# Pooled attention and two MoE layers in one kernel: turning the probabilities with one wide block transpose and moving the blocks by DMA

## Chip, cores and metric

One core of a Trainium2 chip runs the whole program. The metric is the device time of one execution in microseconds; the median of several runs is compared. All times below are microseconds (us) unless they are marked ns.

## What is computed

The reference, cut to what matters (B = 8 batches, H = 8 heads, S = 576 queries, D = 64, pool 8, so 72 pooled keys; 4608 tokens of 512 channels):

```python
k_p = k.reshape(B, H, Sp, pool, D).mean(axis=3)
v_p = v.reshape(B, H, Sp, pool, D).mean(axis=3)
scores = scale * np.matmul(q, k_p.transpose(0, 1, 3, 2))
scores = scores - np.max(scores, axis=-1, keepdims=True)
attn = np.exp(scores)
attn = attn / (np.sum(attn, axis=-1, keepdims=True) + 1e-09)
x = np.matmul(attn, v_p)            # to 4608 x 512
a = x @ w1                          # 512 -> 1024
b = x @ w2
x2 = ((a * b) @ w3) @ w_out         # 1024 -> 512
h = x2 @ w_in                       # 512 -> 2048
g = h * (1.0 / (1.0 + np.exp(-1.702 * h)))
out = g @ w_out2                    # 2048 -> 512
```

## The kernel before

**Numbers.** Every large product is made of three matmuls on rounded parts: each operand is split into a rounded high part and the rest (`split`, L104 on ACT for the high part, L105 on DVE or POOL for the rest), and `mm3` (L114, L115, L116) adds high·high, high·low and low·high. A "slot" `s` holds both parts of a 128x512 piece.

**Phases.** First w3 and w_out are folded into one matrix `wp`. Then the first MoE layer runs in 9 blocks of 512 tokens. A block has 8 steps f (128 hidden channels each): 24 matmuls for a = x@w1 and b = x@w2 into the PSUM banks `wk_70` and `wk_71`, an ACT copy of a (L638), DVE's a*b (L641), its split, and 12 matmuls of an older f into `acc`. At about 770 us the second MoE layer begins (L709), which this change does not touch.

**Attention** is cut into 32 groups n of two heads: four groups make one batch, and group 4b + c gives channel block c of the tokens of batch b. So f = 0 of the first block needs the outputs of groups 0 to 3, one `s` slot each (c = 0 to 3). A group passes through stages: `g0` (kT and qT by block transposes on DVE, L255/L256, and the pooled key sums L258), `g1` (scores on PE L278, row maximum L283 and subtraction L285 on DVE), `g2` (exp on ACT), `g3` (row sum L300, L301, L302, product L303 on DVE, and the turning L314), `g_va` (pooling of v on POOL, L324 to L332, and the load of the next v), `g_vb` (`vm`, `vt`, the two parts of the pooled v: ACT L338, POOL L339), `g4` (the two parts of the turned probabilities, `ph` and `pt`: ACT L368, L370, POOL L369, L372) and `g6` (PE: probabilities by v, eight matmuls of 288 columns; ACT L390 and DVE L391 copy the result as a slot of x).

In the stage `g3` the probabilities lie with 128 queries on the partitions, `s_t[128, 5, 160]`; PE needs the keys on the partitions. The first four groups (n < NPE = 4) are turned on PE in `g4` (L351 on). All others are turned on DVE by 20 block transposes of 32 partitions (L314), whose output goes to other partitions than the input:

```python
            for r in range(5):
                for c in range(4):
                    dst = p0[32 * r:32 * r + 32] if r < 4 else p1[:32]
                    nc.vector.transpose(out=dst[:, :nt, 32 * c:32 * c + 32],
                        in_=s_t[32 * c:32 * c + 32, :nt, 32 * r:32 * r + 32])
```

**What sets the order.** `tick_first` (groups 0 to 3, two ticks apart) and `tick` (four ticks a group) put the stages between the steps of the surrounding loops: the folding of wp first, then two ticks for each f of the blocks. Beside that runs `Conv`, which unpacks and rounds the weights of the second layer: its step (L155) uses ACT (L166, L168), DVE (L169), POOL (L172) and a split (L104, L105, tile `cv`). That written order is not the final one: a scheduler with a timeline of its own sets each engine's sequence when the program is built, so a change of one instruction can move others. Every engine then runs its sequence in order. The raw loads `kr`, `qr` (L229) and `vr`, `vtr` (L249, L250) are DMAs issued by SP. `vr` has one buffer, `vtr` is one fixed tile; `kr` and `qr` share four.

Of the kernel before, what the change touches and what calls it, by code (L numbers as in the profile page):

```python
# [22 lines left out]
def pooled_attention_moe_moe2(  # L23
# [167 lines left out]
    with pa_ctx:  # L191
# [104 lines left out]
        def g3(n):  # L296
# [20 lines left out]

        def g_va(n):

            vr, tr = g_v.pop(n), vtr  # L320
            a = pa.tile([P, 4 * D], F32, name="va", tag="va")
            at = pa.tile([32, 4 * D], F32, name="vat", tag="vat")
            for d, s in ((a, vr), (at, tr)):
                nc.gpsimd.tensor_tensor(out=d, in0=s[:, :4 * D], in1=s[:, 4 * D:], op=ALU.add)  # L324
                nc.gpsimd.tensor_tensor(
                    out=d[:, :2 * D], in0=d[:, :2 * D], in1=d[:, 2 * D:], op=ALU.add)
                nc.gpsimd.tensor_tensor(out=d[:, :D], in0=d[:, :D], in1=d[:, D:2 * D], op=ALU.add)
            vf = pa.tile([P, 2, D], F32, name="vf", tag="vf")
            nc.gpsimd.tensor_tensor(
                out=vf, in0=a[:, :D].unsqueeze(1).to_broadcast([P, 2, D]), in1=mask, op=ALU.mult)  # L330
            vtf = pa.tile([32, D], F32, name="vtf", tag="vtf")
            nc.gpsimd.tensor_scalar_mul(vtf, at[:, :D], 1.0 / POOL)  # L332
# [12 lines left out]
        def g4(n):  # L345
            p0, p1 = g_s.pop(n)
            if n < NPE:
                ps, s_t = banks_of(n), s_of(n)
                p0f, p1f = (t.rearrange("p t c -> p (t c)") for t in (p0, p1))
                for tt in range(4):  # L350
                    nc.tensor.transpose(ps[0][:, sl(tt)], s_t[:, tt, :P], ident)  # L351
                nc.scalar.copy(p0f[:, :T], ps[0])
# [13 lines left out]
            s0 = p0.rearrange("p t c -> p (t c)")[:, :S]  # L366
            s1 = p1.rearrange("p t c -> p (t c)")[:, :S]
            nc.scalar.copy(ph[:, 0], s0)  # L368
            nc.gpsimd.tensor_tensor(out=ph[:, 1], in0=s0, in1=f32(ph[:, 0]), op=ALU.subtract)  # L369
            nc.scalar.copy(pt[:32], s1)  # L370
            nc.scalar.copy(pt[32:64], s1)
            nc.gpsimd.tensor_tensor(out=pt[64:96], in0=s1, in1=f32(pt[:32]), op=ALU.subtract)  # L372
# [756 lines left out]
```

## Time and profile before

| | us |
|---|---|
| median of 3 runs | 1482.65 (1481.53 to 1482.81) |
| the profiled execution | 1480.04 |
| its span in the trace | 1478.3 |
| PE (TensorE matmul) busy | 1437.1 (97%), 6536 instructions |
| PEld (weight loads) | 1188.0 (80%) |
| DVE (VectorE) | 991.5 (67%), 1728 instructions |
| ACT (ScalarE) | 696.6 (47%) |
| POOL (GpSimd) | 491.9 (33%) |
| mean granted TensorE clock | 0.994 of full speed |

The profiled execution took 1480.04 us, of which the trace shows 1478.3; it is 2.6 us shorter than the median of the runs. In a timeline row the columns are the start, the busy time of the row, engine and line, output from input with the shape, and in brackets the idle time of the engine before it with what ended it; x6 means six instructions in one row. In a row of grouped instructions the columns behind the bar are the busy time, the mean ns of one, and the idle time before them. SP's entries (SPq) are the issues of DMAs.

### The profile page before, as it was taken

How to read it: one execution, taken by the hardware profiler on the slowest of the kernel's cores; microseconds unless marked ns; L12 is line 12 of the kernel's file. 1: busy time of each engine (PE TensorE's matmuls, PEld its weight loads, DVE VectorE, ACT ScalarE, POOL GpSimd, SP SyncE). 2: the span in 40 equal slices, each digit the busy share in tenths (PEclk: the TensorE clock that was granted, in tenths of full speed). 3: DMA queues.
4: the chain of work that ended last, by engine and by line, in shares of the span. 5: the costliest groups of instructions: out<-in, count | busy, mean ns of one | idle time of the engine just before them, and what ended most of it. 6: DMA issues, size and time to landing. Idle time of an engine off the chain costs nothing.

```text
span 1478.3 us, 19409 instructions
## 1 busy us (share of the span) xinstructions
PE 1437.1 (97%) x6536; PEld 1188.0 (80%) x6536; DVE 991.5 (67%) x1728; ACT 696.6 (47%) x1212; POOL 491.9 (33%) x589
## 2 busy tenths in 40 slices
PE   5978999999999999999999999999999999999998
PEld 3766888888888888888888887888788888888886
DVE  7889998878787877645636345783559354954554
ACT  6974444434343434366635334652455244634442
POOL 8787865555555555357743200000000000000000
PEclk9989999999999999999999999999999999999999
DMA  9992333323232321089869978877677766785665
GB/s 275 243 227 41 65 81 61 77 49 77 47 75 48 74 41 37 29 295 337 329 230 391 330 240 306 292 213 225 200 237 223 224 199 216 241 237 179 196 213 141
DMA packets 294434, 267.63 MB, mean 181 GB/s; under 512 B 201664, under 2 KB 226240, under 8 KB 294336
## 3 DMA queue, kind: packets, MB, share of 16 engines
q1 hardware_dynamic: 291648, 265.09, 60.0%
q10 hardware_dynamic: 2688, 1.31, 0.3%
q8 instruction: 52, 0.85, 0.2%
q14 instruction: 46, 0.38, 0.1%
HBM read 209.72 MB, written 56.62 MB: 180 GB/s over the span
## 4 chain that ended last, share of the span: by engine, by line
PE 82%; DVE 7%; DMA 5%; ACT 2%; POOL 2%; issue 1%; SPq 1%; DVEq 0%; ACTq 0%; POOLq 0%
PE bk L709 39%; PE wk L114 8%; PE wk L116 8%; PE wk L115 8%; PE acc L114 4%; PE acc L115 4%; PE acc L116 4%; PE wk L278 2%; DMA wud<-wt 2%; DVE s L105 1%; DVE cv L169 1%; PE bk L114 1%; PE bk L115 1%; PE bk L116 1%; POOL cv L172 1%
## 5 line engine op out<-in xcount | busy, mean ns | idle before, releaser
L709 PE MATMUL bk<-xM,st 128*128 128x512 f32 x1140 | 269.1, 390 | 1.8 <-DMA st<-wind 1.3
L709 PE MATMUL bk<-mv,st 128*128 128x512 f32 x1104 | 258.7, 389 | 0.5 <-DMA st<-wud 0.5
L709 PEld LDWEIGHTS bk<-xM,st 128*128 128x128 f32 x1140 | 213.6, 188 | 48.0 <-issue 1.9
L709 PEld LDWEIGHTS bk<-mv,st 128*128 128x128 f32 x1104 | 207.1, 188 | 44.2 <-ACT mv L104 0.9
L114 PE MATMUL wk<-s,s 128*128 128x512 f32 x576 | 227.3, 396 | 6.1 <-DVE a L641 4.1
L116 PE MATMUL wk<-s,s 128*128 128x512 f32 x576 | 225.2, 391 | 0.9 <-DVE s L105 0.9
L115 PE MATMUL wk<-s,s 128*128 128x512 f32 x576 | 225.3, 392 | 0.1
L314 DVE STREAM_TRANSPOSE p<-s_t 32x160 f32<-32x160 f32 (+1 forms) x560 | 178.3, 318 | 10.5
L115 PE MATMUL acc<-s,s 128*128 128x512 f32 x352 | 141.2, 401 | 1.0 <-POOL s L105 0.8
L116 PE MATMUL acc<-s,s 128*128 128x512 f32 x352 | 140.7, 400 | 1.6 <-DVE s L105 1.6
L114 PE MATMUL acc<-s,s 128*128 128x512 f32 x352 | 134.1, 406 | 8.1 <-DVE s L105 5.4
L114 PEld LDWEIGHTS wk<-s,s 128*128 128x128 f32 x576 | 108.5, 189 | 30.1 <-DVE a L641 5.4
L116 PEld LDWEIGHTS wk<-s,s 128*128 128x128 f32 x576 | 108.5, 188 | 23.8 <-DVE s L105 1.1
L115 PEld LDWEIGHTS wk<-s,s 128*128 128x128 f32 x576 | 108.5, 188 | 22.1 <-DVE s L391 0.5
L105 POOL TENSOR_TENSOR s<-a,s 128x512 fp32r<-128x512 f32 x56 | 73.3, 1309 | 155.2 <-ACT s L104 121.4
L105 DVE TENSOR_TENSOR mv<-g,mv 128x1024 fp32r<-128x1024 f32 x80 | 97.8, 1222 | 32.5 <-ACT mv L104 31.0
L104 ACT CAST mv<-g 128x1024 fp32r<-128x1024 f32 x80 | 84.5, 1056 | 71.3 <-PE bk L709 70.8
L172 POOL TENSOR_TENSOR cv<-cv,s 128x512 int32<-128x512 int32 x72 | 100.8, 1408 | 33.6 <-DVE cv L169 24.2
L114 PEld LDWEIGHTS acc<-s,s 128*128 128x128 f32 x352 | 67.9, 194 | 23.3 <-ACT s L104 4.7
L116 PEld LDWEIGHTS acc<-s,s 128*128 128x128 f32 x352 | 67.9, 193 | 15.8 <-DVE s L105 2.7
L115 PEld LDWEIGHTS acc<-s,s 128*128 128x128 f32 x352 | 68.0, 193 | 14.4 <-POOL s L105 2.0
L638 ACT COPY a<-wk 128x512 f32<-128x512 f32 x72 | 42.1, 585 | 68.3 <-PE wk L116 68.1
(188 smaller groups left out, 2344.6 us busy)
## 6 DMA issues: line engine op xcount, KB each, us to landing
st<-wud SPq DMA_DIRECT2D x92, 512.0 KB, 4.3
st<-wind SPq DMA_DIRECT2D x66, 512.0 KB, 4.6
st<-wind SPq DMA_DIRECT2D x84, 256.0 KB, 3.8
s<-in_moe_w_dram SPq DMA_DIRECT2D x32, 512.0 KB, 6.5
wind<-s SPq DMA_DIRECT2D x32, 512.0 KB, 5.5
s<-in_moe_w_out_dram SPq DMA_DIRECT2D x24, 512.0 KB, 6.9
s<-wud SPq DMA_DIRECT2D x20, 512.0 KB, 4.3
kr<-in_k_dram SPq DMA_DIRECT2D x128, 72.0 KB, 2.5
```

What stands on the lines that cost most here:

```text
L104: nc.scalar.copy(dst[:, 0], src)
L105: lo_eng.tensor_tensor(out=dst[:, 1], in0=src, in1=f32(dst[:, 0]), op=ALU.subtract)
L114: nc.tensor.matmul(o, a[:, 0, a_sl], b[:, 0, b_sl], start=first, stop=False)
L115: nc.tensor.matmul(o, a[:, 0, a_sl], b[:, 1, b_sl], start=False, stop=False)
L116: nc.tensor.matmul(o, a[:, 1, a_sl], b[:, 0, b_sl], start=False, stop=last)
L169: nc.vector.tensor_scalar(out=wu, in0=e.bitcast(U32), scalar1=3, scalar2=None, op0=ALU.logical_shift_left)
L172: nc.gpsimd.tensor_tensor(out=w.bitcast(I32), in0=w.bitcast(I32), in1=lo_w.bitcast(I32), op=ALU.add)
L278: nc.tensor.matmul(sc[half][:, i * KW:(i + 1) * KW], qT[:, sl(tt)], mov, start=True, stop=True)
L314: nc.vector.transpose(out=dst[:, :nt, 32 * c:32 * c + 32], in_=s_t[32 * c:32 * c + 32, :nt, 32 * r:32 * r + 32])
L638: nc.scalar.copy(a, pa_)
L709: nc.tensor.matmul(o, w[:, x, m], b[:, y], start=first and n == 0, stop=last and n == 2, skip_group_check=True)
```

## The change

For groups 4 to 31 the 20 transposes of `g3` become one block transpose over all 128 partitions (`turned`, tile `pT`, L324 of the changed kernel), in which each 32x32 block is turned in place of its own 32 partitions. Then 20 DMAs issued by SP (L330), each 32 partitions with rows of 160 or 128 numbers (640 or 512 bytes), take the blocks to the partitions of their keys in `p0` and `p1`. So that a DMA row is one long run, the queries of `qT` are put in another order: `turn_q` turns them by two transposes instead of one (L261), 5x64 and 4x64 columns. `p0` and `p1` are 576 instead of 640 wide. `g_va` adds in place in `vr` and `vtr`: the separate `va` and `vat` are gone, and the load of the next v into the same tiles waits for the last reader of the old one (`vf`, `vtf`) instead of the first addition.

```diff
+        SPANS = ((0, 5), (5, 5), (10, 4), (14, 4))
+
+        def turn_q(n, qr):
+            if n < NPE:
+                nc.vector.transpose(out=qT[:, :S], in_=qr.rearrange("p g d -> p (g d)"))
+                return
+            by_c = qT.rearrange("p (t c j) -> p t c j", c=4, j=32)
+            for c in (0, 2):
+                g, nt = SPANS[c]
+                nc.vector.transpose(
+                    out=by_c[:, :nt, c:c + 2],
+                    in_=qr[:, g:g + 2 * nt].rearrange("p (c t) d -> p t c d", c=2))
+
         def g0(n):
...
-            nc.vector.transpose(out=qT[:, :S], in_=qr.rearrange("p g d -> p (g d)"))
+            turn_q(n, qr)
...
-            p0 = pa.tile([P, TT, P], F32, name="p0", tag="p0")
-            p1 = pa.tile([32, TT, P], F32, name="p1", tag="p1")
+            p0 = pa.tile([P, S], F32, name="p0", tag="p0")
+            p1 = pa.tile([32, S], F32, name="p1", tag="p1")
             g_s[n] = (p0, p1)
             if n < NPE:
                 return
+            turned = pa.tile([P, 5, TT, 32], F32, name="pT", tag="pT")
+            nc.vector.transpose(
+                out=turned.rearrange("p r t j -> p t r j"),
+                in_=s_t.rearrange("p t (r k) -> p t r k", k=32))
             for r in range(5):
-                for c in range(4):
-                    nt = TT if 32 * (c + 1) <= S - (TT - 1) * P else TT - 1
-                    dst = p0[32 * r:32 * r + 32] if r < 4 else p1[:32]
-                    nc.vector.transpose(
-                        out=dst[:, :nt, 32 * c:32 * c + 32],
-                        in_=s_t[32 * c:32 * c + 32, :nt, 32 * r:32 * r + 32])
+                dst = p0[32 * r:32 * r + 32] if r < 4 else p1
+                for c, (g, nt) in enumerate(SPANS):
+                    nc.sync.dma_start(
+                        dst[:, 32 * g:32 * (g + nt)],
+                        turned[32 * c:32 * c + 32, r, :nt].rearrange("p t j -> p (t j)"))
...
-            for d, s in ((a, vr), (at, tr)):
-                nc.gpsimd.tensor_tensor(out=d, in0=s[:, :4 * D], in1=s[:, 4 * D:], op=ALU.add)
...
+            for d in (vr, tr):
+                for w in (4 * D, 2 * D, D):
+                    nc.gpsimd.tensor_tensor(
+                        out=d[:, :w], in0=d[:, :w], in1=d[:, w:2 * w], op=ALU.add)
```

In numbers of rows of the order, DVE has 1450 before and 1202 now, POOL 579 in both, SP 660 before and 942 now. The scheduler also places work of the start differently. Group 3 is the last one that f = 0 of the first block needs; its DVE copies are the two rows L391 from `acc_68` and `acc_69` into `s_815`. DVE's sequence around them before:

```order
L256 STREAM_TRANSPOSE qT<-qr 128x576
L105 TENSOR_TENSOR s_1173<-cv,s_1173 128x512
L258 TENSOR_REDUCE ks<-kT 128x72
L285 TENSOR_TENSOR s_t<-wk_73,nm 128x2x144
L169 TENSOR_SCALAR cv<-cv 128x512
L391 TENSOR_TENSOR s_815<-acc_68,s_815 128x288
L391 TENSOR_TENSOR s_815<-acc_69,s_815 128x224
L283 TENSOR_REDUCE nm<-wk_72 128x6
```

These copies were the 127th and 128th rows of DVE, ahead of everything of group 5 but its kT. The same place in the changed kernel, whose line numbers are its own (L401 is L391 of before, L298 is L285, L313 to L316 are L300 to L303, `s_808` is the slot):

```order
L316 TENSOR_TENSOR s_t<-s_t,nm 128x5x144
L324 STREAM_TRANSPOSE pT<-s_t 128x5x5x32
L298 TENSOR_TENSOR s_t<-wk_72,nm 128x3x144
L298 TENSOR_TENSOR s_t<-wk_73,nm 128x2x144
L169 TENSOR_SCALAR cv<-cv 128x512
L313 TENSOR_REDUCE nm<-s_t 128x10
L401 TENSOR_TENSOR s_808<-acc_68,s_808 128x288
L401 TENSOR_TENSOR s_808<-acc_69,s_808 128x224
L314 TENSOR_SCALAR nm<-nm 128x10
```

The copies are now the 151st and 152nd rows. Ahead of them stand, more than before: 7 of Conv's L169 and 2 of its L105, 2 kT transposes (L255 of before), 1 key sum (L258), one whole qT more (six halves for two whole ones), 2 row sums (L300), 1 product (L303), 1 `pT`, and 6 short ones (L283 and L285 twice, L301, L302). On POOL, `vm` of group 3 (L339) before:

```order
L172 TENSOR_TENSOR cv<-cv,s_963 128x512
L372 TENSOR_TENSOR pt<-p_672,pt 32x576
L329 TENSOR_TENSOR vf<-va,mask 128x128
L332 TENSOR_SCALAR vtf<-vat 32x64
L172 TENSOR_TENSOR cv<-cv,s_1023 128x512
L105 TENSOR_TENSOR s_1248<-cv,s_1248 128x512
L339 TENSOR_TENSOR vm<-vf,vm 128x128
```

And in the changed kernel (L352 is L339 of before, L342 is L329, L345 is L332):

```order
L105 TENSOR_TENSOR s_1585<-cv,s_1585 128x512
L172 TENSOR_TENSOR cv<-cv,s_1145 128x512
L172 TENSOR_TENSOR cv<-cv,s_1170 128x512
L342 TENSOR_TENSOR vf<-vr,mask 128x128
L345 TENSOR_SCALAR vtf<-vtr 32x64
L172 TENSOR_TENSOR cv<-cv,s_1235 128x512
L172 TENSOR_TENSOR cv<-cv,s_1245 128x512
L105 TENSOR_TENSOR s_1660<-cv,s_1660 128x512
L352 TENSOR_TENSOR vm<-vf,vm 128x128
```

Up to `vm` of group 3 POOL now has 39 instead of 31 of Conv's L172 and 11 instead of 7 of its L105. PE's sequence before the first matmuls that read group 3's slot, in the changed kernel, where `wk_70` is a and `wk_71` is b of f = 0:

```order
L114 MATMUL wk_71<-s_698,s_1232 128x512
L115 MATMUL wk_71<-s_698,s_1232 128x512
L116 MATMUL wk_71<-s_698,s_1232 128x512
L114 MATMUL wk_71<-s_808,s_1232 128x512
L115 MATMUL wk_71<-s_808,s_1232 128x512
L116 MATMUL wk_71<-s_808,s_1232 128x512
L114 MATMUL acc_66<-s_1206,s_685 128x512
```

Counted in units of 512 columns, 261 units of PE's queue stand ahead of the first matmul on `s_808`; the matmul of PE's row at 147.50 us in the trace of before has number 386, in both orders.

In the steady part ACT has, of one group (L378 is L368 of before, L648 is L638, L307 the exp of the next group):

```order
L648 COPY a<-wk_70 128x512
L104 CAST s_4214<-a 128x512
L273 COPY kbd<-ks 64x72
L274 COPY kbd<-ks 64x72
L378 CAST ph<-p_4159 128x576
L307 ACTIVATE s_t<-s_t 128x5x144
L648 COPY a<-wk_70 128x512
```

`pT` of this group comes on DVE between the product a*b that precedes the first L648 here and the one that follows it. `ph` is now the reader of the first 16 DMAs of the group; before, it read what L314 had written.

## Rows read from the trace of the kernel before

**Rows 1.** Windows of the span: us, busy of PE, PEld, DVE, ACT, POOL, PEclk, DMA share, GB/s.

```profile
111.00:148.00 37.00, 31.39 (x138) 25.07 (x137) 35.01 (x72) 16.68 (x33) 29.21 (x31) 0.99 0.22 40
...
222.00:592.00 370.00, 370.00 (x1784) 312.93 (x1783) 298.39 (x731) 146.53 (x329) 195.37 (x280) 1.00 0.27 59
```

**Rows 2.** The page's costliest groups: the turning on DVE.

```profile
L314 DVE STREAM_TRANSPOSE p<-s_t 32x160 f32<-32x160 f32 (+1 forms) x560 | 178.3, 318 | 10.5
```

**Rows 3.** Timeline of PE, 107 to 148 us: its late waits and its spacing.

```profile
107.20 0.97 PE L278 MATMUL wk<-kbd,qT 128*128 128x144 f32 x6 [2.06 <-DVE qT L256]
...
115.63 0.50 PE L114 MATMUL wk<-s,s 128*128 128x512 f32 x1 [1.47 <-ACT a L638]
115.97 0.40 PE L115 MATMUL wk<-s,s 128*128 128x512 f32 x1
...
123.69 0.39 PE L116 MATMUL wk<-s,s 128*128 128x512 f32 x1
...
127.23 0.50 PE L114 MATMUL wk<-s,s 128*128 128x512 f32 x1 [2.25 <-DVE a L641]
...
147.50 0.50 PE L114 MATMUL wk<-s,s 128*128 128x512 f32 x1 [1.90 <-DVE a L641]
```

**Rows 4.** Timeline of DVE, 110 to 147 us.

```profile
109.99 0.41 DVE L169 TENSOR_SCALAR cv<-cv 128x512 uint32<-128x512 uint32 x1
110.32 0.74 DVE L391 TENSOR_TENSOR s<-acc,s 128x288 fp32r<-128x288 f32 x2
...
121.27 3.77 DVE L169 TENSOR_SCALAR cv<-cv 128x512 uint32<-128x512 uint32 x1
...
140.07 0.33 DVE L314 STREAM_TRANSPOSE p<-s_t 32x160 f32<-32x160 f32 x1
...
146.75 0.69 DVE L641 TENSOR_TENSOR a<-wk,a 128x512 f32<-128x512 f32 x1
```

**Rows 5.** Groups of DVE, each shape apart, 60 to 260 us.

```profile
L169 DVE TENSOR_SCALAR cv<-cv 128x512 uint32<-128x512 uint32 x19 | 21.5, 1134 | 2.2 <-ACT cv L166 2.2
...
L303 DVE TENSOR_TENSOR s_t<-s_t,nm 128x720 f32<-128x720 f32 x10 | 10.7, 1067 | 0.2
L255 DVE STREAM_TRANSPOSE kT<-kr 128x576 f32<-128x576 f32 x13 | 10.0, 768 | 2.4 <-DMA kr<-in_k_dram 2.3
L105 DVE TENSOR_TENSOR s<-cv,s 128x512 fp32r<-128x512 f32 x8 | 9.8, 1227 | 0.8 <-ACT s L104 0.8
L300 DVE TENSOR_REDUCE nm<-s_t 128x10 f32<-128x720 f32 x10 | 8.9, 892 | 3.0 <-ACT s_t L294 3.0
...
L283 DVE TENSOR_REDUCE nm<-wk 128x4 f32<-128x288 f32 x9 | 4.0, 449 | 1.2 <-PE wk L278 1.2
```

**Rows 6.** Everything of L169, 60 to 260 us: durations in ns.

```profile
L169 DVE TENSOR_SCALAR cv<-cv x19: 389/568/3774, 59.2 to 147.4; 128x512 uint32<-128x512 uint32 x19
```

**Rows 7.** Timeline of POOL: vm of group 3.

```profile
103.64 0.45 POOL L339 TENSOR_TENSOR vm<-vf,vm 128x128 fp32r<-128x128 f32 x1
```

**Rows 8.** Groups of POOL, each shape apart, 60 to 260 us.

```profile
L172 POOL TENSOR_TENSOR cv<-cv,s 128x512 int32<-128x512 int32 x20 | 27.4, 1372 | 4.0 <-DVE cv L169 1.5 <-PE acc L351 0.5 <-DVE s L391 0.5
...
L105 POOL TENSOR_TENSOR s<-cv,s 128x512 fp32r<-128x512 f32 x8 | 10.3, 1284 | 2.4 <-ACT s L104 2.3
```

**Rows 9.** Timeline of ACT and DVE in the steady part.

```profile
441.12 0.57 ACT L638 COPY a<-wk 128x512 f32<-128x512 f32 x1
...
443.47 0.68 DVE L641 TENSOR_TENSOR a<-wk,a 128x512 f32<-128x512 f32 x1
...
450.65 0.59 ACT L638 COPY a<-wk 128x512 f32<-128x512 f32 x1
```

**Rows 10.** Everything of L250 and of L229: issues on SP in ns, and landing.

```profile
L250 SPq DMA_DIRECT2D vtr<-in_v_dram x32: 321/324/403, 17.9 to 561.4; - x32
...
DMA to landing us min/median/max: 1.7/2.3/5.6
...
L229 SPq DMA_DIRECT2D kr<-in_k_dram x128: 311/490/3951, 6.1 to 534.0; - x128
```

More of the change, by code (lines that the diff above doesn't have):

```diff
@@ L309, in g3 @@
                 return
+            turned = pa.tile([P, 5, TT, 32], F32, name="pT", tag="pT")
+            nc.vector.transpose(
+                out=turned.rearrange("p r t j -> p t r j"),
+                in_=s_t.rearrange("p t (r k) -> p t r k", k=32))
             for r in range(5):
[L311 to L316 removed]
+                dst = p0[32 * r:32 * r + 32] if r < 4 else p1
[3 more added lines that the diff above has]
+                        turned[32 * c:32 * c + 32, r, :nt].rearrange("p t j -> p (t j)"))
         def g_va(n):
             vr, tr = g_v.pop(n), vtr
[L321 to L327 removed]
+            for d in (vr, tr):
+                for w in (4 * D, 2 * D, D):
+                    nc.gpsimd.tensor_tensor(
+                        out=d[:, :w], in0=d[:, :w], in1=d[:, w:2 * w], op=ALU.add)
             vf = pa.tile([P, 2, D], F32, name="vf", tag="vf")
             nc.gpsimd.tensor_tensor(
[L330 removed]
+                out=vf, in0=vr[:, :D].unsqueeze(1).to_broadcast([P, 2, D]), in1=mask, op=ALU.mult)
             vtf = pa.tile([32, D], F32, name="vtf", tag="vtf")
[L332 removed]
+            nc.gpsimd.tensor_scalar_mul(vtf, tr[:, :D], 1.0 / POOL)
             g_v[n] = (vf.rearrange("p a d -> p (a d)"), vtf)
@@ L348, in g4 @@
                 ps, s_t = banks_of(n), s_of(n)
-                p0f, p1f = (t.rearrange("p t c -> p (t c)") for t in (p0, p1))
                 for tt in range(4):
                     nc.tensor.transpose(ps[0][:, sl(tt)], s_t[:, tt, :P], ident)
-                nc.scalar.copy(p0f[:, :T], ps[0])
+                nc.scalar.copy(p0[:, :T], ps[0])
                 w = S - T
@@ L357, in g4 @@
                         ps[1][:32, w + tt * P:w + (tt + 1) * P], s_t[:, tt, P:], ident)
-                nc.scalar.copy(p0f[:, T:S], ps[1][:, :w])
-                nc.scalar.copy(p1f[:, :3 * P], ps[1][:32, w:w + 3 * P])
+                nc.scalar.copy(p0[:, T:S], ps[1][:, :w])
+                nc.scalar.copy(p1[:, :3 * P], ps[1][:32, w:w + 3 * P])
                 nc.tensor.transpose(ps[0][:32, :P], s_t[:, 3, P:], ident)
                 nc.tensor.transpose(ps[0][:32, P:P + w], s_t[:w, 4, P:], ident[:w, :w])
-                nc.scalar.copy(p1f[:, 3 * P:S], ps[0][:32, :P + w])
+                nc.scalar.copy(p1[:, 3 * P:S], ps[0][:32, :P + w])
             ph = pa.tile([P, 2, S], F32R, name="ph", tag="ph")
@@ L365, in g4 @@
             g_s[n] = (ph, pt)
[L366 to L372, printed above, removed]
+            nc.scalar.copy(ph[:, 0], p0)
+            nc.gpsimd.tensor_tensor(out=ph[:, 1], in0=p0, in1=f32(ph[:, 0]), op=ALU.subtract)
+            nc.scalar.copy(pt[:32], p1)
+            nc.scalar.copy(pt[32:64], p1)
+            nc.gpsimd.tensor_tensor(out=pt[64:96], in0=p1, in1=f32(pt[:32]), op=ALU.subtract)
         def g6(n):
```

## Prediction

> **What bounds the kernel.** I read the page first, then windows, then the timeline of PE for its waits, then the engines that it waits for. From 222 to 592 us PE is busy in all of the 370 us [rows 1], while DVE has 298 of them. So in this stretch, in which most groups run, no time can be saved outside PE, and the change takes nothing from PE: the number of its instructions is the same. The largest cost that the change removes, 178.3 us of turning on DVE in 560 instructions [rows 2], is therefore cover and not path. It is different at the start: from 111 to 148 us PE has 31.4 of 37 us [rows 1], with DVE at 35.0 of 37. There PE waits, and the rows say for what: 2.06 us at 107.20 for qT, 1.47 at 115.63, 2.25 at 127.23 and 1.90 at 147.50 us, the last two for DVE's product L641 [rows 3]. These four, 2.06 + 1.47 + 2.25 + 1.90 = 7.7 us, are all that a relieved DVE could give back here. The prediction is decided between 103 and 160 us.
>
> **The change part by part.**
>
> *Turning in the steady part.* 20 transposes of 318 ns (6.4 us) [rows 2] become one of 800 columns: the 576-column one takes 768 ns [rows 5], so 768 x 800/576 = 1.07 us. DVE gets 28 x (6.4 - 1.07) = 149 us free; on the path this is 0, since PE is full without it. qT by halves moves the same columns; 28 extra instructions on an engine with slack: 0.
>
> *The 20 DMAs a group.* Their way is new: SP issues, blocks land, then ACT's `ph`. Bounds for one issue are the small load L250 (0.32 us) and the strided L229 (median 0.49 us), landing 2.3 us [rows 10]. I take 0.32, because the rows to be moved are whole runs, as in L250: 20 x 0.32 + 2.3 = 8.7 us; with 0.49 it is 12.1. In the changed order `ph` stands ahead of the second ACT copy L638 after `pT`. If ACT waits in `ph`, the next exp and that L638 are queued behind it, and PE waits for its bank. The time until then: L638 comes every 9.53 us (441.12 to 450.65) and the product 2.35 us after it [rows 9]; `pT` ends about 3 us after the product (my estimate: row sum 0.89, product 1.07, `pT` 1.07 [rows 5]). So 2 x 9.53 - 2.35 - 3 = 13.7 us are there: 8.7 and 12.1 both fit, cost 0. It begins to cost above (13.7 - 2.3)/20 = 0.57 us an issue. If this cover went, the price would be a stall for each of 28 groups (third rival).
>
> *The v in place.* The next v load waits for `vf`, `vtf` instead of the first addition, a few POOL instructions later, with the rest of a period of two f, 19 us, ahead for a 2.3 us landing [rows 9, 10]. On SP this wait stands behind the 20 DMAs and ahead of the loads of q and k, which have four buffers. Cost 0, and no gain.
>
> *The start: what the scheduler moved.* The first block's f = 0 needs the four slots of groups 0 to 3. Before, DVE wrote the slot of group 3 at 110.32 us [rows 4], and POOL's `vm` for it stood at 103.64 [rows 7]. In the new order both stand later.
>
> POOL: 8 more L172 at 1372 ns and 4 more L105 at 1284 [rows 8], 11.0 + 5.1 = 16.1 us, so `vm` at about 119.8.
>
> DVE, ahead of the slot's copies, with the durations of rows 5: 7 L169 x 1.134 = 7.9; 2 L105 x 1.227 = 2.5; 2 kT, one qT and one key sum of the same width, 4 x 0.768 = 3.1; 2 row sums x 0.892 = 1.8; one product 1.07; one `pT` 1.07; six short ones, taken as the 288-column L283, 6 x 0.449 = 2.7. Together 20.1 us. Neighbours overlap in the records: L169 at 109.99 with 0.41 us reaches 0.08 beyond the next start at 110.32 [rows 4]; about 0.07 each for two dozen, so -1.7. The copies start at 110.3 + 18.4 = 128.7 and end 0.74 later [rows 4], at 129.5. That is behind POOL's chain, so DVE decides.
>
> PE has by then done what stands ahead of the first matmul on that slot, 261 units of 512 columns, and nothing can be taken from behind it. From there to unit 386, which before started at 147.50 after its last large wait, are 125 units. At full clock PE spaces them by (123.69 - 115.97)/34 = 0.227 us [rows 3]: 28.4 us. So unit 386 comes at 129.5 + 28.4 = 157.9 instead of 147.5: **+10.4 us**. Conv's pieces are then done earlier, DVE is lighter behind (the transposes at 140.07 that hold up the product at 146.75 [rows 4] are gone), and I count no further wait. PE is full afterwards, so a late start is never made up.
>
> *Sum:* 1480.04 (the profiled execution) + 10.4 + 0 + 0 = 1490.4. The median of the runs lies 2.6 us above the profiled one, so **1493.0**.
>
> *Bounds of the unknown term.* L169 takes from 0.389 to 3.774 us [rows 6]. At 0.389 each the seven cost 5.2 us less: +5.2, 1487.8. If two of the seven take 3.77 (as the one at 121.27 [rows 4]), it is 5.3 more: +15.7, 1498.3. I take the mean, because this mixture of long and short ones comes from the same place.
>
> *A rule weighed.* The L169 at 121.27 took 3.77 us, ten times the shortest [rows 4, 6]. The Trainium skill, page "SBUF — State Buffer", section "SBUF: two separate sides", says that DVE and GpSimd share a port pair which is locked for a whole instruction, by whichever of them starts first, for DVE operations in a two-port mode or with two SBUF inputs. By this rule L169 pays where POOL is dense, which more L172 ahead of group 3's slot would make likelier: the sum would go to the upper bound, by the mean alone it stays at +10.4. The trace agrees with a spread of 389 to 3774 ns, but does not tell which port held it. The rule speaks against a gain of POOL, too: a transpose has one input, so removing 560 of them need not free anything there.
>
> **Rivals.**
>
> *R1, faster: DVE's relief reaches PE.* If the new places cost nothing, because DVE runs ahead of its old times by more than 18.4 us of work that it no longer does or never waited for, the four waits vanish: 1480.04 - 7.7 + 2.6 = **1475**. For it: DVE is at 35.0 of 37 us there [rows 1] and two of the four waits name L641, which stood behind transposes. Against it: the transposes of groups 4 and 5 lie mostly after the slot's copies at 110.32, so their removal cannot bring those forward, and the added 20 us lie ahead of them. The point of decision: copies of group 3 ending before about 119 us (157.9 - 147.5 = 10.4 earlier than 129.5). Chance 0.18.
>
> *R2, no change: both cancel.* The slot comes some 7 us late instead of 18, say, because L169 takes 0.4 to 0.6 and POOL's and DVE's orders fill holes; vanished waits pay for the late start: within 3 us of **1482.6**. For it: the median of L169 is 0.568, half its mean [rows 6]. Against it: from 111 to 148 us DVE had 2 us of holes in 37 [rows 1]. Chance 0.22.
>
> *R3, much slower: the DMA path is the new wait.* It decides above 0.57 us an issue. At 0.65, say, the way is 15.3 against 13.7 us: 1.6 x 28 groups = 46, about **1530**. For it: L229's longest issues are 3.95 us and its median 0.49 [rows 10]; SP has 560 more DMAs. Against: the DMA share is 0.27 in this stretch [rows 1]. Chance 0.04.
>
> That the change doesn't do what it says is no rival here: the order shows one `pT` and 20 DMAs a group.
>
> **How the numbers follow.** The forecast (+10.4, own range 1488 to 1498) has the rest, 0.56. A measurement of this kernel can tell about 0.2%, 3 us, from no change. Faster is R1, 0.18; same is R2, 0.22; slower is the forecast and R3, 0.60. The range runs from 1477, which takes in R2 and the better edge of what cancels, to 1499, the upper bound; it leaves out most of R1 and R3, about 0.2.
>
> **What would show it.** Right: in the changed trace PE is full from about 165 us on; DVE's last copy of group 3 is at 127 to 133 us, and PE has one long wait in front of f = 0's last channel, ended by it; `vm` at about 120; `pT` near 1.07 us; issues on SP 0.3 to 0.5 us and ACT's `ph` not waiting on DMA with PE idle. Wrong: the copies of group 3 before 119 us, which would take away the forecast's mechanism; PE waits after 222 us that end on ACT's L638 behind `ph`, which would be R3; PE's total wait between 74 and 185 us smaller than before, which would be R1.

## The result, and the profile after

| | before | changed |
|---|---|---|
| median of the runs, us | 1482.7 | 1504.6 (1500.1 to 1505.4, 4 runs) |
| the profiled execution, us | 1480.04 | 1505.33 |
| its span | 1478.3 | 1503.6 |
| PE busy | 1437.1 | 1444.4 |
| DVE busy | 991.5 | 859.9 |

The changed kernel is slower: ratio 1.0138, 95% interval 1.0113 to 1.0164, some 22 us. Forecast was 1493.0, slower by 10.4 us, with a range of 1477 to 1499; the median lies above it. DVE lost 132 us of work and the time did not gain by it. The windows of the changed kernel, in the columns of [rows 1]:

```profile
111.00:148.00 37.00, 27.66 (x100) 21.83 (x101) 21.50 (x37) 14.74 (x32) 32.86 (x44) 0.68 0.32 66
...
222.00:592.00 370.00, 366.20 (x1746) 306.77 (x1745) 196.27 (x358) 139.40 (x320) 194.95 (x276) 1.00 0.36 76
```

From 111 to 148 us PE is now less busy (27.7 against 31.4 us), at a lower granted clock (0.68 against 0.99) and with DVE idle for 15 us. From 222 to 592 us it is no longer full: the trace shows holes of 3.8 us, where [rows 1] had none. So there are two losses, not one. The timeline of PE shows the first:

```profile
105.85 1.00 PE L291 MATMUL wk<-kbd,qT 128*128 128x144 f32 x6 [3.59 <-DVE s L401]
...
121.90 0.61 PE L390 MATMUL acc<-ph,vm 128*128 128x288 f32 x1 [2.01 <-ACT vm L351]
...
128.16 0.85 PE L392 MATMUL acc<-ph,vm 128*128 128x288 f32 x2 [4.93 <-POOL vm L352]
...
130.05 1.22 PE L114 MATMUL wk<-s,s 128*128 128x512 f32 x2 [0.56 <-ACT s L400]
...
132.14 0.63 PE L115 MATMUL wk<-s,s 128*128 128x512 f32 x1
132.57 0.63 PE L116 MATMUL wk<-s,s 128*128 128x512 f32 x1
```

Lines are those of the changed kernel (from 121.90 us on, L390 to L392 are group 3's products by `vm` and L393 those by `vt`; L401 are the copies to x). PE waits for `vm` of group 3, then for its slot, and afterwards its matmuls are 0.43 us apart for a while instead of 0.227 [rows 3]. The granted clock was 0.50 to 0.51, the lower of its two levels, from 111.78 to 134.80 us, and 1.00 behind that; from 105.85 to 111.78 us, ahead of it, PE was busy for 2.4 of 5.9 us. What is late is POOL's `vm`, at 127.66 us instead of 103.64 [rows 7]; DVE's copies follow it at 130.32 instead of 110.32 [rows 4]:

```profile
120.28 0.46 POOL L342 TENSOR_TENSOR vf<-vr,mask 128x128 f32<-128x128 f32 x1
...
127.66 0.45 POOL L352 TENSOR_TENSOR vm<-vf,vm 128x128 fp32r<-128x128 f32 x1
```

```profile
130.32 0.75 DVE L401 TENSOR_TENSOR s<-acc,s 128x288 fp32r<-128x288 f32 x2
```

The second loss shows in the chain that ended last: before, it was PE for 82% of the span; now SP's issues of the new DMAs stand in it.

```profile
PE 55%; SPq 17%; DMA 8%; POOL 8%; DVE 5%; issue 3%; ACT 3%; ACTq 0%; POOLq 0%; DVEq 0%
PE bk L719 40%; SPq L330 16%; DMA p<-pT 3%; PE wk L116 2%; PE wk L115 2%; PE wk L114 2%; POOL pt L382 2%; POOL vr L339 2%; PE acc L114 1%; PE acc L116 1%; POOL s L105 1%; DMA wud<-wt 1%; POOL vtr L339 1%; PE acc L115 1%; DVE s L105 1%
```

SP's own rows, everything of L330 and then one group in the timeline of SP, with this group's `pT` on DVE and its `ph` on ACT behind it:

```profile
L330 SPq DMA_DIRECT2D p<-pT x560: 507/589/1727, 127.8 to 652.9; - x187
...
DMA to landing us min/median/max: 1.7/1.8/3.7
```

```profile
392.70 12.54 SPq L330 DMA_DIRECT2D p<-pT  x20
405.34 0.53 SPq L249 DMA_DIRECT2D vr<-in_v_dram  x1
405.96 0.37 SPq L250 DMA_DIRECT2D vtr<-in_v_dram  x1
406.39 2.24 SPq L229 DMA_DIRECT2D kr<-in_k_dram  x4
408.67 3.34 SPq L229 DMA_DIRECT2D qr<-in_q_dram  x4
412.11 12.54 SPq L330 DMA_DIRECT2D p<-pT  x20
```

```profile
388.57 1.01 DVE L324 STREAM_TRANSPOSE pT<-s_t 128x800 f32<-128x800 f32 x1 [5.38 <-DMA p<-pT]
...
404.15 0.68 ACT L378 CAST ph<-p 128x576 fp32r<-128x576 f32 x1 [4.19 <-DMA p<-pT]
```

An issue takes 0.589 us at the median, more than either bound that the prediction took (0.32 and 0.49 [rows 10]); twenty take 12.54 us, 0.627 each. SP is full from group to group: `pT` ends at 389.58, and SP, busy with older loads, comes to its blocks at 392.70. Over groups 10 to 31 the first issue comes 2.65 us behind the end of `pT` at the median, the 16 issues that `ph` needs take 10.4 us, and `ph` starts 13.9 us behind `pT`. `pT` has one buffer, and DVE waited 5.38 us there for the DMAs of the group before; in 11 of the 28 groups such waits add up to 36.9 us.

**Where the time goes, along PE's queue.** PE's matmuls are the same in both kernels, so the loss can be read as a lag: the time at which PE has done so many units of 512 columns (columns of PE's timeline rows, added up in order), minus that time in the kernel before. It is good to about 1 us, and each value is that of one execution. In the changed kernel the lag is 13.1 us at unit 400 (162 us), 12.8 at unit 500, then 13.8 at 1500, 15.5 at 2000, 19.2 at 2300, 23.1 at 3000 (782 us, the end of the first layer), and 25.3 at the end of this execution. So: 13 us at the start, 10 in the first layer, 2 in the second.

### The profile page after: what moved, and what is told of

It is laid out like the page before. It is cut to its first block, busy times and chain, and to the rows that moved or that the text cites. A ratio compares the mean times of both kernels' runs of the same rounds, so it can differ in the third digit from the quotient of the medians.

```text
span 1503.6 us, 19862 instructions
## 1 busy us (share of the span) xinstructions
PE 1444.4 (96%) x6536; PEld 1189.7 (79%) x6536; DVE 859.9 (57%) x1224; ACT 694.6 (46%) x1212; POOL 495.5 (33%) x589
## 4 chain that ended last, share of the span: by engine, by line
PE 55%; SPq 17%; DMA 8%; POOL 8%; DVE 5%; issue 3%; ACT 3%; ACTq 0%; POOLq 0%; DVEq 0%
PE bk L719 40%; SPq L330 16%; DMA p<-pT 3%; PE wk L116 2%; PE wk L115 2%; PE wk L114 2%; POOL pt L382 2%; POOL vr L339 2%; PE acc L114 1%; PE acc L116 1%; POOL s L105 1%; DMA wud<-wt 1%; POOL vtr L339 1%; PE acc L115 1%; DVE s L105 1%
## 5 line engine op out<-in xcount | busy, mean ns | idle before, releaser
L116 PE MATMUL acc<-s,s 128*128 128x512 f32 x352 | 139.6, 397 | 2.1 <-DVE s L105 2.1
L114 PE MATMUL acc<-s,s 128*128 128x512 f32 x352 | 131.4, 400 | 9.9 <-DVE s L105 5.9
L115 PE MATMUL acc<-s,s 128*128 128x512 f32 x352 | 139.6, 396 | 1.2 <-POOL s L105 1.1
L116 PEld LDWEIGHTS wk<-s,s 128*128 128x128 f32 x576 | 109.1, 189 | 24.5 <-DVE s L105 3.2
L105 DVE TENSOR_TENSOR mv<-g,mv 128x1024 fp32r<-128x1024 f32 x80 | 97.7, 1222 | 33.4 <-ACT mv L104 31.9
L172 POOL TENSOR_TENSOR cv<-cv,s 128x512 int32<-128x512 int32 x72 | 98.9, 1381 | 48.4 <-DVE cv L169 26.9
L379 POOL TENSOR_TENSOR ph<-p,ph 128x576 fp32r<-128x576 f32 x32 | 46.4, 1451 | 164.9 <-ACT ph L378 145.7
L105 POOL TENSOR_TENSOR s<-a,s 128x512 fp32r<-128x512 f32 x56 | 72.5, 1295 | 46.4 <-ACT s L104 45.5
L116 PEld LDWEIGHTS acc<-s,s 128*128 128x128 f32 x352 | 67.1, 191 | 16.3 <-DVE s L105 3.0
L115 PEld LDWEIGHTS acc<-s,s 128*128 128x128 f32 x352 | 67.2, 191 | 15.3 <-POOL s L105 2.3
L378 ACT CAST ph<-p 128x576 fp32r<-128x576 f32 x32 | 21.6, 675 | 102.8 <-DMA p<-pT 102.8
```

The costliest lines, as they stand in the source:

```text
L105: lo_eng.tensor_tensor(out=dst[:, 1], in0=src, in1=f32(dst[:, 0]), op=ALU.subtract)
L114: nc.tensor.matmul(o, a[:, 0, a_sl], b[:, 0, b_sl], start=first, stop=False)
L115: nc.tensor.matmul(o, a[:, 0, a_sl], b[:, 1, b_sl], start=False, stop=False)
L116: nc.tensor.matmul(o, a[:, 1, a_sl], b[:, 0, b_sl], start=False, stop=last)
L172: nc.gpsimd.tensor_tensor(out=w.bitcast(I32), in0=w.bitcast(I32), in1=lo_w.bitcast(I32), op=ALU.add)
L378: nc.scalar.copy(ph[:, 0], p0)
```

## Experiments

The theories, by the letters that the expectations use. S: the start is late because of what the in-place v does to the order (later: because the next v load waits longer). D: the DMA way makes the whole loss, the start too. Q: SP's queue is full, and its backlog makes the growth behind the start. L: the way from `pT` by the DMAs to `ph` is too long. To make room, the mask of the v pooling is 1 instead of 64 wide in e4 to e6, e9 to e11, e13, e16 and e17. All lags below are of the profiled execution, against that of the kernel before.

| run | median us (range) | ratio, 95% interval | lag at unit 350 | 400 | 500 | 3000 |
|---|---|---|---|---|---|---|
| changed | 1504.6 (1500.1 to 1505.4) | 1.0138, 1.0113 to 1.0164 | 14.9 | 13.1 | 12.8 | 23.1 |
| e1 v in place alone | 1498.2 (1496.4 to 1499.4) | 1.0108, 1.0093 to 1.0123 | 21.6 | 19.4 | 18.2 | 16.4 |
| e2 DMAs from group 8 | 1500.3 (1497.5 to 1500.7) | 1.0117, 1.0099 to 1.0135 | 21.9 | 19.7 | 18.5 | 17.8 |
| e3 six DMAs by DRAM | 1503.2 (1498.1 to 1506.8) | 1.0140, 1.0112 to 1.0168 | 19.4 | 17.3 | 17.1 | 13.8 |
| e4 vr apart, vtr in place | 1506.8 (1501.7 to 1508.7) | 1.0162, 1.0139 to 1.0185 | 17.1 | 15.3 | 14.3 | 24.1 |
| e5 v apart | 1508.8 (1506.8 to 1517.5) | 1.0185, 1.0154 to 1.0216 | 6.9 | 4.6 | 4.2 | 34.6 |
| e6 v apart, six DMAs | 1486.3 (1485.7 to 1490.2) | 1.0036, 1.0022 to 1.0051 | 6.4 | 4.8 | 3.9 | 3.3 |
| e7 as e3, other DRAM space | 1502.3 (1496.9 to 1504.0) | 1.0134, 1.0117 to 1.0151 | 18.7 | 16.3 | 16.2 | 13.0 |
| e8 DMAs for groups 4 to 7 | 1499.6 (1496.9 to 1500.2) | 1.0108, 1.0093 to 1.0123 | 17.1 | 15.5 | 14.5 | 16.6 |
| e9 as e1, two v buffers | 1495.9 (1494.1 to 1498.5) | 1.0097, 1.0076 to 1.0117 | 2.9 | 8.9 | 8.1 | 12.6 |
| e10 e5 again | 1505.7 (one run) | | 6.0 | 3.7 | 3.3 | 24.5 |
| e11 e5, q loads on ACT | 1500.6 (1498.3 to 1503.0) | 1.0127, 1.0106 to 1.0148 | 8.1 | 5.5 | 5.0 | 21.6 |
| e12 v as before, six DMAs, q on ACT | 1493.0 (1490.4 to 1494.6) | 1.0079, 1.0060 to 1.0099 | 9.8 | 7.7 | 7.3 | 7.7 |
| e13 two v buffers, six DMAs | 1486.7 (1482.3 to 1487.7) | 1.0023, 1.0009 to 1.0036 | 3.0 | 0.9 | 0.5 | 2.0 |
| e14 changed, q and k on ACT | 1527.4 (1525.4 to 1529.0) | 1.0300, 1.0285 to 1.0316 | 20.0 | 18.3 | 17.2 | 47.4 |
| e15 changed again | 1507.4 (one run) | | 13.6 | 12.0 | 12.8 | 24.4 |
| e16 spare DMAs behind | 1500.6 (1499.8 to 1502.0) | 1.0116, 1.0100 to 1.0133 | 14.7 | 13.2 | 16.2 | 17.1 |
| e17 spare DMAs between | 1513.3 (1512.0 to 1515.4) | 1.0203, 1.0187 to 1.0218 | 14.7 | 13.0 | 12.0 | 28.8 |

### e1: only the v pooling in place

```diff
 (the kernel before)
-            a = pa.tile([P, 4 * D], F32, name="va", tag="va")
-            at = pa.tile([32, 4 * D], F32, name="vat", tag="vat")
-            for d, s in ((a, vr), (at, tr)):
...
+            for d in (vr, tr):
+                for w in (4 * D, 2 * D, D):
+                    nc.gpsimd.tensor_tensor(
+                        out=d[:, :w], in0=d[:, :w], in1=d[:, w:2 * w], op=ALU.add)
```

> The kernel before with only the v pooling in place (no wide transpose, no DMAs of the probabilities, 20 DVE transposes as before). Theory S (start): the in-place v alone makes the scheduler place group 3's slot late (39 of Conv's POOL additions ahead of vm instead of 31), and PE is 13 us late at unit 400 as in the changed kernel, with no growth behind: 1482.7 + 13 = 1495, 1492 to 1499. Rival D (the DMA way makes the whole loss, the start included): 1482.7, within 3 us.

15.4 us of loss with none of the transposes and DMAs touched, and no growth after the start. The smallest part of the change makes most of the loss. Rival D is out. Its rows say how. Loads of v on SP for groups 2 and 3, first before, then in e1 (the row of 100.63 us is e1's load for group 3), and e1's `vm` of group 3 on POOL:

```profile
70.57 0.45 SPq L249 DMA_DIRECT2D vr<-in_v_dram  x1
...
88.43 0.44 SPq L249 DMA_DIRECT2D vr<-in_v_dram  x1
```

```profile
81.31 1.37 SPq L249 DMA_DIRECT2D vr<-in_v_dram  x1
...
100.63 0.44 SPq L249 DMA_DIRECT2D vr<-in_v_dram  x1
```

```profile
127.66 0.45 POOL L336 TENSOR_TENSOR vm<-vf,vm 128x128 fp32r<-128x128 f32 x1
```

The load that has to wait for `vf` is issued 11 and 12 us later, and `vm` of group 3 is 24 us late, at the very time of the changed kernel. It is its place in SP's order that is later, not a wait at run time: `vf` of group 2 ended at 93.26 in e1, 7 us ahead of group 3's load, and SP issued loads of q and k in between. The other 12 us of `vm` lie on POOL, between the first addition of this v and `vm`, where the scheduler put more of Conv's work. Both are effects of the order that it made of the in-place additions.

### e2 and e8: the wide transpose and its DMAs for some groups only

```diff
 (the changed kernel; e8: NPE <= n < 8)
-            if n < NPE:
+            if not (n >= 8):
                 nc.vector.transpose(out=qT[:, :S], in_=qr.rearrange("p g d -> p (g d)"))
...
+            if not (n >= 8):
+                for r in range(5):
+                    for c in range(4):
...
+                        nc.vector.transpose(
+                            out=dst[:, :nt, 32 * c:32 * c + 32],
+                            in_=s_t[32 * c:32 * c + 32, :nt, 32 * r:32 * r + 32])
+                return
```

> The changed kernel, but groups 4 to 7 are turned by the 20 DVE transposes; groups 8 to 31 by the wide transpose and DMAs. Theory S + Q (Q: SP's queue is full with 20 issues of about 0.62 us a group): the start is as late as in the changed kernel, and the growth behind is there for 24 of 28 groups: 1500 to 1505. Rival D: the start's loss of 13 us goes with the DMAs of groups 4 to 7: about 1491.

> The changed kernel, but only groups 4 to 7 use the wide transpose and DMAs; groups 8 to 31 are turned by 20 DVE transposes. Theory S: the start is as late as in the changed kernel, 13 to 17 us, and nothing is lost behind: 1496 to 1500. Theory Q alone (loss from SP's issues in all groups): 1486.

The start is late in both, whether or not groups 4 to 7 use DMAs: it does not come of the DMAs. In e8 hardly anything is lost behind the start (2 us), as expected. In e2 it was expected, and is not there (18.5 to 17.8), though 24 groups have the DMAs. The total (1500.3) lay in the range that was expected, for another reason: the start was 6 us later. The growth is thus no plain price of so much a group. Nor is it a plain price of a full queue: SP spends 90% of the time from 222 to 560 us in issues in e2 as in the changed kernel, and PE has no wait from 222 to 782 us. e16 and e17 come back to it.

### e3, e7: six DMAs through DRAM instead of twenty

```diff
-            for r in range(5):
-                dst = p0[32 * r:32 * r + 32] if r < 4 else p1
-                for c, (g, nt) in enumerate(SPANS):
-                    nc.sync.dma_start(
...
+            keys = pt_d[n % 2]          # e7: a part of x2_d[NB - 1]
+            for c, (g, nt) in enumerate(SPANS):
+                nc.sync.dma_start(
+                    keys[:, :, 32 * g:32 * (g + nt)].rearrange("r k x -> k r x"),
+                    turned[32 * c:32 * c + 32, :, :nt].rearrange("p r t j -> p r (t j)"))
+            nc.sync.dma_start(p0, keys[:4].rearrange("r k x -> (r k) x"))
+            nc.sync.dma_start(p1, keys[4])
```

> The changed kernel with 6 instead of 20 DMAs a group: four writes of the turned blocks to DRAM, two reads of long rows (2304 bytes) back into p0 and p1. The same bytes go twice. Theory Q: what counts is SP's time for issues (20 x 0.62 = 12.4 us becomes 6 x 0.6 = 3.6 us), so the 10 us of growth after 222 us go and only the late start stays: about 1495, 1492 to 1498. Rival L (the length of the DMA way, landing and all, not SP's queue): two landings one behind the other make it 1503 or more.

> As e3 (6 DMAs a group through DRAM), but with the DRAM space taken from a tile that is written later anyway. In e3 PE was 14 us late up to 830 us and lost 11 more in the second layer, waiting for weights from DRAM. If that came of the shifted DRAM tiles, the second layer is now as in the kernel before and the time is about 1482.7 + 14 = 1497; if it comes of chance or of the start, 1500 to 1507 again.

The growth is gone in both (17.1 to 13.8, 16.2 to 13.0). But the totals missed: e3 loses 12 us more in the second layer, where PE waits for weights from DRAM (lag 25.4 at unit 5800), e7 4 us in the profiled execution, which was its fastest. The other space for the blocks did not settle it. Nor was the rival put well: the way through DRAM is not longer. From the end of `pT` to `ph` it takes 6.8 us at the median of 22 groups in e7, against 13.9 in the changed kernel, since 14 issues fewer outweigh one landing more. So these two runs cut both SP's load and the length of the way.

### e4, e5, e6: v pooled apart again

```diff
 (e4: vr alone; e5: both; e6: e5 with the six DMAs of e7)
+            a = pa.tile([P, 4 * D], F32, name="va", tag="va")
+            if n < NPE:
+                at = pa.tile([P, 5, TT, 32], F32, name="vat", tag="pT").rearrange(
...
+            else:
+                at = pa.tile([32, S], F32, name="vat", tag="p1")[:, :4 * D]
```

> The changed kernel with the v pooling of vr again into a tile of its own, so that the next v load waits only for the first addition; vtr stays in place, and the mask is 1 instead of 64 wide to make room. Group 3's vm has 31 instead of 39 of Conv's POOL additions ahead of it, its DVE copies 144 instead of 150 rows. Theory S: PE's late start shrinks from 13 to 5 to 8 us, the growth after 222 us stays: 1497 to 1501. Rival D, or a start set by DVE's order alone: 1503 to 1506.

> The changed kernel with v pooled outside vr and vtr again (room made by a 1 wide mask and by tiles that share space), so only the wide transpose, the qT halves and the DMAs are left of the change. In its order vm of group 3 has 31 L172 and 7 Conv splits ahead of it, as before the change, and its DVE copies stand at row 138 (127 before, 151 in the changed kernel). Theory S: PE is late by 0 to 5 us at unit 400 instead of 13; theory Q: the 10 us of growth from SP's full queue stay. Together about 1495, 1491 to 1498. If the start were made by the DMAs: 1503 or more.

> As e5, and in addition the blocks go through DRAM with 6 DMAs a group, the DRAM space being taken from a tile that is written later anyway, so that no other DRAM tile moves. Theory S + Q: start late by 0 to 5 us, no growth behind: 1483 to 1488. If the wide transpose is of use at the start, 1476 to 1480.

e4 missed: 15 us late still. The tail `vtr` is pooled in place there and its load waits as in the changed kernel; PE now waits for `vt` (2.8 us at 125.27) and then for the slot. Half of the v in place is as bad as all. In e5 both are apart and the start is 4 us late, as theory S has it; but the growth is 30 us instead of 10, so the total missed by far. (The profiled execution was the slowest of e5, 9 us above its median; e10 is the same kernel again.) Here `vat` shares space with `p1`, which ties v pooling to the DMAs' end. e6 has the same sharing with six DMAs: no growth, 1486.3, in the expected range. The pair e5 and e6 differs only in the DMAs; the start is the same, the growth is 30 us (21 in e10) against none, and the medians lie 22.5 us apart.

### e9: in place, but with two buffers

```diff
 (e1, and)
+        vrs = [pa.tile([P, POOL * D], F32, name=f"vr{i}") for i in range(2)]
+        vtrs = [pa.tile([32, POOL * D], F32, name=f"vtr{i}") for i in range(2)]
...
-            g_v[n] = pa.tile([P, POOL * D], F32, name="vr", tag="vr")
+            g_v[n] = vrs[n % 2]
```

> As e1 (the kernel before with the v pooling in place), but with two buffers each for vr and vtr (room from a 1 wide mask and from vf and vtf lying in vr and vtr), so that the load of the next v need not wait for vf of this group. If the late start comes of that wait (in e1 the v loads of groups 2 and 3 are issued at 81.3 and 100.6 us, before the change at 70.6 and 88.4), they are early again, vm of group 3 is at about 104 and the time is 1480 to 1486. If adding in place or the new order as such costs the 15 us: 1495 to 1500.

What was to be shown is there: group 3's load on SP and its `vm` on POOL are early,

```profile
79.89 0.61 SPq L251 DMA_DIRECT2D vr<-in_v_dram  x1
```

```profile
103.29 0.92 POOL L338 TENSOR_TENSOR vm<-vr,vm 128x128 fp32r<-128x128 f32 x1
```

and the lag at unit 350 is 2.9 us where e1 has 21.6. But the total missed, and lies in the range of the rival: the scheduler's order is again another, and two rows of DVE and one of PE show a new wait.

```profile
142.59 6.65 DVE L316 STREAM_TRANSPOSE p<-s_t 32x160 f32<-32x160 f32 x20
149.27 0.69 DVE L640 TENSOR_TENSOR a<-wk,a 128x512 f32<-128x512 f32 x1
```

```profile
150.02 0.79 PE L114 MATMUL wk<-s,s 128*128 128x512 f32 x1 [6.21 <-DVE a L640]
```

The 20 transposes stand ahead of the product, and PE waits 6.2 us for it. These are what the wide transpose takes away, which e13 tries. They are not alone: ahead of them a TENSOR_SCALAR of 10 columns took 4.18 us on DVE, some 3.8 more than usual (its row stands further down).

### e10, e11, e12, e14: other engines for the loads

```diff
 (e11 and e12; in e14 q and k from group 8 on; e10 is e5 unchanged)
-            load_blocks(g_q[n], q, b, hp)
+            load_blocks(g_q[n], q, b, hp, nc.scalar if n >= 6 else nc.sync)
```

> Not changed against e5: a second look at it beside e11, 1504 to 1512.

> As e5 (20 DMAs a group, 1508.8 us, PE 30 us late behind 160 us of growth), but from group 6 on the four loads of q are issued by ACT: SP has 4 issues of 0.5 us, 2 us a group, less, the way of the probabilities is as long as before. Theory Q (SP's queue is full): the growth goes or shrinks below 8 us, 1485 to 1495. Rival: the tiles that share space, or the length of the way, make the growth of e5: 1503 or more.

> What the theories leave of the change: wide transpose, six DMAs a group through DRAM, v pooling as in the kernel before (room because p0 shares a tile with pT), q loads from group 6 on issued by ACT. Theory S + Q: no late start, no growth: 1479 to 1487, within 0.3% of the kernel before, since PE is full behind 150 us either way; the relief of DVE can give at most the 7.7 us of PE's waits from 107 to 148 us. Below 1478 the relief is worth more than that.

> The changed kernel, with the loads of q and k from group 8 on issued by ACT: of 28 issues and more a group (20 of the probabilities at 0.63 us, 8 of q and k at 0.5 us, v and x2) SP loses 4 us in 18.7; the row of 20 issues stays as long. Theory Q (SP's queue is full, its backlog makes the waits): the growth after unit 700 falls from 11 us to 0 to 3: 1494 to 1499. Theory L (the row of 20 issues, 12.5 us, plus landing is longer than the time until ph is wanted): the growth stays, 8 us or more: 1502 to 1508.

e10 shows that the growth of e5 differs between executions: 21 instead of 30 us. e11 still grows by 17 us, so a little room on SP does not end it; its total, 1500.6, lies between the two ranges. In e14 SP stands idle for up to 8 us a group, and the growth is 30 us, the total 1527.4 and above both ranges: theory Q as stated there failed. But theory L has no better hold on these two: their way from `pT` to `ph` is 12.4 us at the median, shorter than in e2, which does not grow. ACT, which now issues loads itself, may be a cause of its own; that was not tested apart, and in e12 the issues of q on ACT made no growth. e12 has none, but starts 7 us late, so that its total (1493.0) missed too: the order of ACT and DVE at the start is one more that none of the theories foresaw.

### e13, e15: both causes out, and the changed kernel again

> Both causes removed at once: v pooled in place but in two buffers for vr and vtr (as e9), and the wide transpose with six DMAs a group through DRAM (as e7), p0 sharing a tile with pT for room. In e9 the slot of group 3 was early (PE 3 us late at unit 350 instead of 22), but PE then waited 6.2 us at 150 us for a product behind 20 transposes on DVE (142.6 to 149.2 us); these are now one. Theory S + Q: PE 0 to 4 us late at unit 400, no growth: 1480 to 1487. If the late start has a cause besides the v loads: 1492 or more.

> The changed kernel once more, to see how far start and growth repeat: PE 12 to 14 us late at unit 400 and 8 to 14 us more at unit 3000.

e13 is e9's buffers with e7's DMAs, `p0` sharing a tile with `pT`. The lag is 0.9 us at unit 400 and 2.0 at unit 3000: with early v loads and a short way, both losses are gone. Nothing is gained either: the window from 222 to 592 us is full again, and the median is 1.0023 times that of before (1.0009 to 1.0036, so still some 3 us slower; in the profiled execution 3 to 4 us arise in the second layer). So no version beat the kernel before. e15 repeats the changed kernel's two losses: 12.0 and 24.4.

### e16, e17: SP's load against the length of the way

```diff
 (e7, and in e16 behind the two reads, in e17 ahead of them)
+            for i in range(14):
+                nc.sync.dma_start(
+                    spare[:, i % 4], turned[:32, i % 5, 0])
```

> As e7 (six DMAs a group through DRAM), and 14 more small DMAs a group from pT into a spare tile that nothing reads, two ahead of the reads and 12 behind them: SP has 20 issues again, the way of the probabilities stays short. Theory Q (SP's full queue): PE's lag grows by 8 us or more between units 500 and 3000, 1503 or more. Theory L (the length of the way): no growth, PE 13 to 17 us late throughout, 1496 to 1503.

> As e16, but all 14 spare DMAs stand between the four writes and the two reads: SP has the same 20 issues, and the way of the probabilities holds all of them and two landings. Theory L: growth of 8 us or more, more than in the changed kernel, 1505 or more. Theory Q: the same as e16.

These DMAs move data that nothing reads. SP's rows of a group, first e16, then e17:

```profile
392.65 1.94 SPq L332 DMA_DIRECT2D x2d<-pT  x4
394.64 1.14 SPq L338 DMA_DIRECT2D spare<-pT  x2
396.06 0.36 SPq L335 DMA_DIRECT2D p<-x2d  x1
396.52 0.36 SPq L336 DMA_DIRECT2D p<-x2d  x1
396.93 7.48 SPq L338 DMA_DIRECT2D spare<-pT  x12
```

```profile
401.56 1.94 SPq L332 DMA_DIRECT2D x2d<-pT  x4
403.55 8.80 SPq L336 DMA_DIRECT2D spare<-pT  x14
412.40 0.58 SPq L338 DMA_DIRECT2D p<-x2d  x1
413.08 0.37 SPq L339 DMA_DIRECT2D p<-x2d  x1
```

Twenty issues a group in both, and SP hardly idle. In e16 the reads come early, and the lag between units 500 and 3000 goes from 16.2 to 17.1. In e17 they stand behind all the others: 12.0 to 28.8, and the totals lie 12.7 us apart. The way from `pT` to `ph` is 9.2 us at the median in e16 and 15.2 in e17. So a full SP alone costs little; what costs is that the blocks come late. Theory Q is out as it was put. A full queue counts by what it adds to the way, though: in the changed kernel 2.65 of the 13.9 us pass before SP comes to the first block, and e16 has 2.2 us of this kind without growth, since the rest of its way is short.

Theory L also fits e2. From the end of `pT` to the start of `ph` the median of 22 groups is 13.9 us in the changed kernel and 12.8 in e2; the prediction had worked out 13.7 us as the time that is there. That e2's way is the shorter by 1 us was read from the trace, and not tested further. The length of the way does not settle everything: e11 and e14 grow at 12.4 us, and e5 grows by 30 us at 15.0 where e17 grows by 17 at 15.2.

One rival was not tested. `pT`, `p0` and `p1` have one buffer each, so slow DMAs also hold up DVE at the next `pT`, and what stands behind it. These waits of DVE add up to 36.9 us in the changed kernel, 26.5 in e17, 20.6 in e11, 7.9 in e2, 0.8 in e16 and none in e7 and e13; of the runs that grow by 10 us or more only e14 (1.9 us) has hardly any. Whether PE was late by way of ACT's `ph` or by way of DVE no run tells apart; a run with a second buffer for `pT` could.

## Why the prediction was wrong

The runs show 13 us at the start where 10.4 were forecast, 10 in the first layer where 0 were, and 2 in the second where 0 were.

- **The sign and the place of the first loss** were right: PE is full from about 165 to 222 us, one long wait stands ahead of f = 0's last channel, and what comes late there is never made up. `vm` was forecast for 119.8 and came at 127.66; the copies for 128.7, and began at 130.32.
- **The step "The v in place ... Cost 0, and no gain" failed.** It priced the wait in the steady part, where 19 us are there, and not at the start, where the v load of each group is on the way to its `vm`. e1 shows this one edit to cost 15 us alone; e9 shows `vm` back at its old place once the load need not wait. These 15 us are not to be added to the 10.4: the late places that the start's term counted are the effect of this edit.
- **The step "what the scheduler moved"** took the late places as they stood and named no cause. The sum of 20.1 us of DVE's work was near by chance: DVE idled 15 us of the 37, and POOL's `vm` ended last, not DVE. L169 took 0.726 us at the mean of its 19 between 60 and 260 us, not 1.134.
- **The 125 units at 0.227 us** were mis-sized: the first matmuls after the long waits were 0.43 us apart. From PE's new start at 130.05 to 134.80 us it did ten units, which at 0.227 are 2.3 us: 2.5 us lost. With this and a start 0.5 us later than forecast, 10.4 becomes 13.4; the lag at unit 400 is 13.1.
- **The step "The 20 DMAs a group ... cost 0" failed**, and by it the sum is 10 us short. An issue took 0.589 us at the median and 0.627 in a row, not 0.32. The upper bound was the fault: the median of a load from DRAM was taken as an upper bound for a transfer between partitions that no row showed. The count was wrong as well, since `ph` needs 16 of the 20: 16 x 0.627 + 1.8 = 11.8 us at most (the 1.8 us of landing count from the start of an issue), which would still fit into the 13.7 that the prediction had. What it left out is that SP is not free when `pT` ends; with 2.65 us of backlog the way is 13.9 us. By its own sum, 20 x 0.627 + 1.8 = 14.3 us, it would have come near by chance. The point of decision, 0.57 us an issue, is not borne out either: e2 is above it and does not grow.
- **R3** named the DMA way as the new wait, at a chance of 0.04, and this was so; but by its sum 28 x (14.3 - 13.7) = 17 us would be lost, and 10 were. Nor did the loss come where R3 looked for it. Of PE's ten waits from 222 to 782 us, 6.2 us together, five end on `ph` or the product for `pt`, 1.79 us on a slot's copy, and only one, 0.81 us, on L648.
- **R1** foresaw 1475 by DVE's relief, and no run came below the kernel before. e13 has not e9's wait of 6.2 us for L640, but the order differs there in more than the transposes, and the 4.18 us of one short operation were part of that wait; that the relief itself is worth anything is not shown.
- **The rule weighed**, that DVE and GpSimd share a locked port pair (the Trainium skill, "SBUF — State Buffer", "SBUF: two separate sides"), was to push the sum to its upper bound by way of L169. It did not: the longest L169 from 60 to 260 us took 1.49 us. Long ones came elsewhere: in e9 a TENSOR_SCALAR of 128x10, 0.375 us at the mean before, took 4.18 us while POOL worked without a break:

```profile
137.01 4.18 DVE L303 TENSOR_SCALAR nm<-nm 128x10 f32<-128x10 f32 x1
```

  That fits the rule if this operation runs in a two-port mode; no run here shows the mode, or which port held it.

Open: the second layer takes 2 us more in the changed kernel, 2 to 12 in the runs with DRAM in between. PE waits for weights there; e7 did not settle why. Why the growth differs so much between runs with 20 DMAs (none in e2, 10 in the changed kernel, 30 in e5 and e14) stays open too. How the written program turns into this order at the start (e4, e12) was not resolved further than the v loads.

## What to carry to other kernels

Saving memory by working in place makes the next load wait for the last reader instead of the first: price that wait where the pipeline starts, one group behind the other, and not where it runs full. Here it cost 15 us through the order that the scheduler made of it. When a transfer between partitions is cut into many DMAs of one queue, the consumer waits for what stands ahead of them in the queue, then for the count that it needs times the issue time, then for the landing; compare this with the time until the consumer stands in its engine's order, with the issue time of a transfer of the same kind. And the 132 us of work taken from DVE, which hid beside a full PE, were worth nothing.

## What was not expected of the hardware

- An issue of a DMA between two SBUF tiles took SP 0.589 us (32 rows of 512 or 640 bytes) and 0.583 us (32 rows of 128 bytes, e16) at the median, never under 0.507, whereas the read back of `p1` from DRAM took 0.37 (e16) and the small load of v 0.32 [rows 10]. The size of the rows made next to no difference.
- The landing was quick, 1.8 us at the median from the start of the issue. Of the changed kernel's way of 13.9 us, 10.4 were issues and 2.65 the wait until SP came to the first.
